# Pooled attention and a gated layer on one core: the first tile written in another order, value loads ahead of queries, the gate ahead of the second batch's value sums

## The chip, the cores and the metric

The kernel runs on one core of a Trainium2 chip. The metric is the device time of one execution in microseconds; lower is better. Three runs of the kernel before took 976.91 to 977.65, with a median of 977.51. The engines are TensorE (PE in the profile; its weight loads are PEld), VectorE (DVE), ScalarE (ACT), GpSimd (POOL) and SyncE (SP), which here issues all DMAs in the order of its list.

## What is computed

Eight batches of eight heads with 576 queries of 64 numbers. Keys and values are first averaged in groups of eight, to 72 each; the attention's output is the input x (4608 tokens of 512) of a gated layer with 1536 hidden columns.

```python
def _attn_ref(q, k, v):
    k_p = k.reshape(B, H, Sp, pool, D).mean(axis=3)
    v_p = v.reshape(B, H, Sp, pool, D).mean(axis=3)
    scores = scale * np.matmul(q, k_p.transpose(0, 1, 3, 2))
    scores = scores - np.max(scores, axis=-1, keepdims=True)
    attn = np.exp(scores)
    attn = attn / (np.sum(attn, axis=-1, keepdims=True) + 1e-09)
    return np.matmul(attn, v_p)

def _moe_ref(x, w_gate, w_val, w_out):
    g = x @ w_gate
    silu = g * (1.0 / (1.0 + np.exp(-g)))
    val = x @ w_val
    return silu * val @ w_out
```

## The kernel before

The tokens are worked through in nine tiles of 512. Tile 0 is batch 0's first 512 tokens; tile 1 is its last 64 and 448 of batch 1. A tile is made of pieces of at most 128 tokens of one batch: pieces 0 to 3 are tile 0, pieces 4 to 8 tile 1. The gated layer goes over the hidden columns in 12 chunks of 128. Products are taken in split precision: x and the gate and value weights each as a high and a low half-precision part, three products instead of one.

Tiles from 1 on are laid out by a planner (`hidden_tiles`), which puts attention work of later tiles between the matmuls of the present one. Tile 0 has no earlier work to hide behind, so its order, with that of all loads, weight preparation and attention of pieces 0 to 8, is written out by hand in `ORDER`: a list of job names with an index, recorded under a manual schedule, so that each engine gets its instructions in the order of the list, and waits for data by semaphores alone. One step (the last projection, O14) is issued behind it.

The jobs that this text names, with the engine that does them:

- Loads, on SP: `Lk`, `Lr` keys of batch 0 and 1 (halves, 576 KB), `Lv`, `Lu` values of batch 0 and 1 (parts 0 and 1 of the main rows, part 2 the rest, 512 KB), `Lq` queries of a piece (256 KB), `Lw` a weight chunk (1536 KB). `T` is a DMA transpose of a piece's softmax. `La` loads a part of batch 2.
- Attention of a piece: `S` scores (PE, L536), `M` subtract the row maximum (DVE, L552, L553), `E` exponential (ACT, L560), `Na` row sums (DVE), `N` normalise (POOL, L587), `H` and `P` high and low half (ACT, POOL), `T`, `Y` values (PE, L646 to L649), `X` and `Z` high and low half of x (ACT L669, DVE L673).
- Keys and values of a batch: `Kp`, `Kq`, `Kb` key sums (DVE, POOL L272 to L274); `Vp`, `Vq` value sums of batch 0 and 1 (PE, L381, into one PSUM bank); then `Vm` the largest (DVE), `Vo` its sum over rows (PE), `Vs` the scale, `R` ratios, `Vg`, `Vh` (DVE) and `Vx`, `Vf` (ACT) split them into halves.
- A weight chunk: `a` shift (DVE, L202), `b` sign (ACT, L212, or for three chunks DVE), `c` absolute value (ACT, L218), `d` join (DVE, L222), `e` sums (ACT, L233), `f` their total (PE, L181, L182), `g` scale (DVE), `h`, `j` high halves of gate and value weight (ACT, L248), `i`, `k` low halves (DVE, L253), `l`, `m` the output weight (ACT, POOL), `un` factors (POOL).
- The gated layer, step by step: `G` gate and `V` value side (PE, L797 to L799, 12 matmuls each), `t` tanh, `u` and `v` products, `w` cast, `y` low part, `O` projection (PE). Steps 0 to 2 are chunks 0 to 2 for the first 256 tokens, 3 to 5 the same chunks for the other 256, 6 to 14 chunks 3 to 11 for all 512. So steps 0 to 2 need x of pieces 0 and 1 alone.
- `ZERO` clears the four accumulators with zero matmuls (L937); `D` followed by a number is as many matmuls with zeros that change nothing (L941).

Small buffers turn: two for weight chunks as loaded (a third load waits until `d` of the first is done), two for queries, three for joined weights and batch parts, and two PSUM banks for everything of attention beside scores of pieces 0 to 3. Batch 1's value sums hold one of these two banks until they are split.

Of the kernel before, what the change touches and what calls it, by code (L numbers as in the profile page):

```python
# [34 lines left out]


ORDER = """
Lk0 Lq0 Lk1 Lv2 Lv1 Lv0 Lq1 Lw0 Kp0 Kb0 Kp1 CZ Lw1 Lr0 Lu0 S0 Vp0 M0 Lq2 Vp2 E0 Na0 S1
a0 N0 b0 Vp1 Lq3 M1 Vm0 a1 Vo0 E1 Vs0 Kq0 R0 Vx0 H0 Vh0 Vq0 b1 Vg0 S2 Lr1 Na1 Lu2 P0 S3
Lq4 Vf0 M2 N1 T0 Lq5 H1 Kq1 Vq2 E2 c0 Y0 Lu1 Na2 X0 d0 Z0 Lw2 P1 l0 Vq1 e0 M3 T1 m0 f0  # L40
c1 N2 g0 ZERO Vm1 h0 Vo1 E3 d1 H2 j0 Vs1 Lw3 P2 e1 R1 D10 Y1 Vg1 Vx1 T2 a2 X1 l1 Vh1 un0
b2 m1 Z1 D8 f1 g1 k0 S4 i0 a3 G0 h1 Lq6 j1 M4 un1 c2 V0 k1 t0 Y2 E4 d2 b3 Lw4 i1 Na3 u0
l2 N3 D8 G1 v0 X2 w0 c3 y0 m2 Z2 O0 t1 d3 H3 V1 e2 u1 Lw5 P3 v1 l3 f2 g2 e3 T3 a4 h2 f3
j2 g3 un2 i2 w1 j3 y1 h3 k2 D4 O1 b4 i3 G2 k3 a5 V2 b5 t2 Y3 c4 u2 m3 X3 v2 Vf1 Z3 d4 G3
w2 c5 y2 Lw6 un3 t3 O2 l4 d5 e4 V3 u3 Lw7 m4 l5 f4 G4 v3 g4 w3 m5 y3 j4 O3 e5 k4 V4 Na4
t4 c6 u4 N4 f5 G5 v4 g5 h4 w4 a6 S5 H4 y4 t5 un5 b6 i4 V5 Lq7 u5 P4 M5 O4 G6 v5 T4 un4
a7 w5 c7 y5 d6 E5 O5 t6 j5 u6 Lw8 S6 e6 k5 Na5 V6 h5 Lq8 M6 l6 N5 H5 i5 f6 G7 v6 E6 P5
g6 w6 h6 y6 j6 T5 a8 O6 t7 u7 un6 Na6 c8 S7 b8 b7 V7 M7 i6 G8 E7 v7 d7 w7 Y4 y7 Lw9 N6
e7 O7 t8 d8 H6 X4 u8 Lw10 m6 Y5 e8 Z4 V8 l8 k6 X5 m8 l7 Z5 c9 f7 f8 v8 m7 G9 g7 w8 g8 j7
un7 y8 j8 un8 a9 h7 V9 t9 Na7 b9 u9 N7 O8 v9 i7 k7 w9 H7 y9 G10 k8 c10 d9 h8 V10 t10  # L50
Lw11 i8 e9 u10 La0 a10 l9 f9 O9 v10 m9 g9 w10 h9 y10 j9 un9 O10 i9 b10 k9 La1 a11 G11
b11 d10 V11 t11 Pa0 l10 u11 e10 G12 v11 w11 y11 c11 m10 f10 O11 g10 t12 d11 h10 j10 u12
l11 un10 V12 k10 e11 i10 m11 La2 G13 v12 P6 w12 y12 f11 O12 t13 g11 P7 T6 u13 h11 j11 T7
k11 S8 Ln i11 un11 Pa2 V13 M8 La3 E8 G14 La4 Na8 v13 N8 w13 y13 Y6 Pa3 t14 u14 V14 X6
Pa4 H8 La5 P8 O13 v14 La6 w14 T8 y14 Z6 Pa5 Y7 Pa6 Y8 X7 Z7 X8 La7 Pa1 Z8 Pa7 A A
"""
# [1087 lines left out]
```

## Time and profile before

| | us |
|---|---|
| median of 3 runs | 977.51 |
| the profiled execution | 975.54 |
| its span, first to last instruction | 973.8 |
| PE busy in the span | 939.7 |
| DVE busy | 566.0 |
| ACT busy | 461.2 |
| POOL busy | 241.3 |

The profile is one execution. Its span is 1.74 us shorter than that execution's own time, and the execution is 1.97 us below the median of the runs. PE is busy 97% of the span; busy time alone does not say where the rest lies, so the rows below look at stretches.

### The profile page before, as it was taken

To read this page: it belongs to the slowest core of one execution; us is meant where nothing else is said; L and a number is where in the kernel's file an instruction comes from. 1 tells how busy PE (TensorE), PEld (TensorE's weight loads), DVE (VectorE), ACT (ScalarE), POOL (GpSimd) and SP (SyncE) were. 2 spreads that over 40 slices of the span, in tenths; PEclk is the share of its full clock that TensorE was granted. 3 is DMA by queue.
4 is the path that set the end of the run, shared out by engine and by line. 5 is a ranking of instruction groups with operands and counts; after the bars stand their busy time and mean duration, and the time that the engine had idled before them with its cause. 6 is when DMAs were issued, how large, how long until landed. Compare 5 with 4: busy or idle time off the path is not lost.

```text
span 973.8 us, 14306 instructions
## 1 busy us (share of the span) xinstructions
PE 939.7 (97%) x5486; PEld 498.4 (51%) x5486; DVE 566.0 (58%) x1005; ACT 461.2 (47%) x864; POOL 241.3 (25%) x327
## 2 busy tenths in 40 slices
PE   5779999799999999999999999999999999999998
PEld 4657545354555555554555555554545555444443
DVE  6788877667766675586446675674444454323222
ACT  3898883245554553544254544552454443222222
POOL 4533336035226230521025211620121201000000
PEclk9899999999999999999999999999999999999999
DMA  9855426246437342653047232840231222001001
GB/s 349 237 154 208 154 109 171 80 115 186 92 109 211 102 83 79 187 127 82 13 88 235 57 70 87 251 86 15 77 83 43 71 66 55 11 1 44 0 1 44
DMA packets 155524, 103.02 MB, mean 106 GB/s; under 512 B 113216, under 2 KB 141888, under 8 KB 153920
## 3 DMA queue, kind: packets, MB, share of 16 engines
q1 hardware_dynamic: 155456, 102.11, 37.3%
q8 instruction: 43, 0.70, 0.3%
q14 instruction: 25, 0.20, 0.1%
HBM read 67.63 MB, written 9.44 MB: 79 GB/s over the span
## 4 chain that ended last, share of the span: by engine, by line
PE 87%; DMA 6%; POOL 2%; ACT 2%; issue 1%; DVE 1%; SPq 0%; POOLq 0%; DVEq 0%; ACTq 0%
PE gv L797 18%; PE gv L798 18%; PE gv L799 18%; PE acc L824 10%; PE acc L830 9%; PE acc L831 9%; DMA pt<-half 2%; DMA kr<-k_rows 1%; DMA in<-v_rest 1%; DMA in<-k_rows 1%; PE ps L542 1%; PE ps L658 1%; PE ps L543 1%; PE ps L659 1%; DMA k<-k_rows 1%
## 5 line engine op out<-in xcount | busy, mean ns | idle before, releaser
L797 PE MATMUL gv<-x,wgv_h 128*128 128x512 f16 (+1 forms) x888 | 332.0, 374 | 3.8 <-ACT x L669 1.8
L798 PE MATMUL gv<-x,wgv_h 128*128 128x512 f16 (+1 forms) x888 | 331.8, 374 | 1.3 <-DVE x L673 1.3
L799 PE MATMUL gv<-x,wgv_l 128*128 128x512 f16 (+1 forms) x888 | 331.9, 374 | 0.5 <-DVE wgv_l L253 0.5
L810 DVE SCALAR_TENSOR_TENSOR hf<-hf,gv 128x512 f32<-128x512 f32 (+1 forms) x111 | 74.1, 668 | 171.6 <-ACT hf L807 171.3
L807 ACT ACTIVATE hf<-gv,un 128x512 f32<-128x512 f32 (+1 forms) x111 | 74.8, 674 | 193.9 <-PE gv L799 193.9
L1076 ACT CAST hh<-gv 128x512 fp32r<-128x512 f32 x96 | 56.3, 586 | 227.2 <-DVE gv L815 227.2
L831 PE MATMUL acc<-hb,wo_l 128*128 128x512 bf16 x384 | 145.5, 379 | 0.0
L824 PE MATMUL acc<-hh,wo_h 128*128 128x512 f32 (+1 forms) x444 | 139.5, 436 | 0.0
L799 PEld LDWEIGHTS <-wgv_l 128*128 128x128 f16 x888 | 87.0, 98 | 102.2 <-issue 1.7
L798 PEld LDWEIGHTS <-wgv_h 128*128 128x128 f16 x888 | 87.0, 98 | 98.1 <-issue 4.7
L797 PEld LDWEIGHTS <-wgv_h 128*128 128x128 f16 x888 | 87.4, 98 | 94.3
L1080 DVE TENSOR_TENSOR hl<-gv,hh 128x512 bf16<-128x512 f32 x96 | 66.3, 691 | 111.0 <-ACT hb L1077 111.0
L525 POOL TENSOR_TENSOR box<-qt,box 64x512 f16<-64x512 f32 (+1 forms) x60 | 64.0, 1067 | 227.8 <-issue 160.9
L815 DVE SCALAR_TENSOR_TENSOR gv<-gv,un,hf 128x512 f32<-128x512 f32 (+1 forms) x111 | 82.3, 741 | 63.0 <-PE gv L799 62.3
L830 PE MATMUL acc<-hl,wo_b 128*128 128x512 bf16 x288 | 109.8, 381 | 0.0
L824 PEld LDWEIGHTS acc<-hh,wo_h 128*128 128x128 f32 x444 | 83.2, 191 | 24.2 <-ACT hh L969 0.3
L630 POOL TENSOR_TENSOR half<-sc,half 128x512 f16<-128x512 f32 (+1 forms) x30 | 34.7, 1158 | 215.8 <-ACT half L620 193.6
L831 PEld LDWEIGHTS <-wo_l 128*128 128x128 bf16 x444 | 43.7, 98 | 37.9
L1077 ACT CAST hb<-gv 128x512 bf16<-128x512 f32 x96 | 56.8, 591 | 0.0
L830 PE MATMUL acc<-hl,wo_h 128*128 128x512 bf16 (+1 forms) x156 | 56.7, 368 | 0.0
L830 PEld LDWEIGHTS <-wo_b 128*128 128x128 bf16 x288 | 28.3, 98 | 42.2 <-issue 16.6
L523 ACT ACTIVATE qt<-qt,inv 128x512 f32<-128x512 f32 (+1 forms) x60 | 40.9, 682 | 0.0
(143 smaller groups left out, 1121.5 us busy)
## 6 DMA issues: line engine op xcount, KB each, us to landing
ws<-w_all SPq DMA_DIRECT2D x12, 1536.0 KB, 7.1
qt<-q_twice SPq DMA_DIRECT2D x48, 256.0 KB, 3.2
out_t<-ob SPq DMA_DIRECT2D x36, 256.0 KB, 2.3
in<-k_rows SPq DMA_DIRECT2D x12, 576.0 KB, 3.9
in<-q_rows SPq DMA_DIRECT2D x12, 576.0 KB, 5.2
in<-v_main SPq DMA_DIRECT2D x12, 512.0 KB, 4.3
in<-v_rest SPq DMA_DIRECT2D x12, 512.0 KB, 5.7
qt<-q_rows SPq DMA_DIRECT2D x8, 256.0 KB, 4.3
```

Of the source, the lines that this page charges most:

```text
L525: nc.gpsimd.tensor_sub(o[rows], qt[rows], o[rows])
L797: nc.tensor.matmul(o, wh, x["h"][:, j, a:e], start=(j == 0), stop=False)
L798: nc.tensor.matmul(o, wh, x["l"][:, j, a:e], start=False, stop=False)
L799: nc.tensor.matmul(o, wl, x["h"][:, j, a:e], start=False, stop=(j == NJ - 1))
L807: nc.scalar.activation(hf, gate, AF.Tanh, scale=un[:, c, 0:1])
L810: nc.vector.scalar_tensor_tensor(out=hf, in0=hf, scalar=1.0, in1=gate, op0=ALU.add, op1=ALU.mult)
L815: nc.vector.scalar_tensor_tensor(out=out, in0=val, scalar=un[:, c, 2:3], in1=hf, op0=ALU.mult, op1=ALU.mult)
L824: nc.tensor.matmul(o, wo_h[:, c, js], hh[:, :n], start=begin, stop=False)
L830: nc.tensor.matmul(o, wo[:, c, js], hl[:, :n], start=False, stop=False)
L831: nc.tensor.matmul(o, wo_l[:, c, js], hb[:, :n], start=False, stop=end)
L1077: nc.scalar.copy(hb[:, :n], val)
L1080: nc.vector.tensor_sub(hl[:, :n], val, hh[:, :n].bitcast(F32))
```

## The change

`ORDER` is written anew. It holds the same jobs, with one more (`Vc1`) and 24 idle matmuls instead of 30. The scores of piece 1 and batch 0's value loads come earlier, queries and one half of batch 1's keys (`Lr0`) later; pieces 0 and 1 are normalised and split before batch 1's key sums; the first gate (`G0`) stands ahead of the second batch's scale and split, and of the first score of piece 4. `Vc1` (`v_keep`) copies batch 1's value sums from PSUM to SBUF on ScalarE; what reads them afterwards reads the copy.

```diff
 ORDER = """
-Lk0 Lq0 Lk1 Lv2 Lv1 Lv0 Lq1 Lw0 Kp0 Kb0 Kp1 CZ Lw1 Lr0 Lu0 S0 Vp0 M0 Lq2 Vp2 E0 Na0 S1
-a0 N0 b0 Vp1 Lq3 M1 Vm0 a1 Vo0 E1 Vs0 Kq0 R0 Vx0 H0 Vh0 Vq0 b1 Vg0 S2 Lr1 Na1 Lu2 P0 S3
+Lk0 Lk1 Lv0 Lq0 Lq1 Lv2 Lw0 Lv1 Kp0 Kb0 Kp1 CZ Lw1 S0 Lu0 Lu1 S1 Lq2 M0 Vp0 Lq3 E0 Na0
+Vp2 N0 H0 M1 Vp1 a0 E1 Vm0 b0 Na1 Vo0 Vs0 N1 R0 Vq0 P0 Vg0 H1 Vf0 Vq1 Lr1 a1 T0 Vx0 P1
...
+    def v_keep(b):
+        kept = at.tile([P, NJ + 2, D], F32, name="vkept", bufs=1)
+        nc.scalar.copy(kept, state["vs", b])
+        state["vs", b] = kept
...
-            "Vm": v_largest, "Vo": v_total, ...
+            "Vc": v_keep, "Vm": v_largest, "Vo": v_total, ...
```

What this does to each engine is seen from the instructions in order. TensorE at its start, before (L381 are value sums, `v` batch 0's main part, `vr` any other part; L536 are scores, eight matmuls in 64 rows of keys each):

```order
L536 MATMUL ps<-ksum_122,qt 128x72 x8
L381 MATMUL ps<-v_145,unit 128x128 x8
L381 MATMUL ps<-vr,unit 128x128 x8
L536 MATMUL ps<-ksum_122,qt 128x72 x8
L381 MATMUL ps<-v_145,unit 128x128 x8
L181 MATMUL ps<-least,ones 128x1
L182 MATMUL ps<-mx_240,ones 128x1
```

and after:

```order
L541 MATMUL ps<-ksum_122,qt 128x72 x16
L381 MATMUL ps<-v_141,unit 128x128 x8
L381 MATMUL ps<-vr,unit 128x128 x8
L381 MATMUL ps<-v_141,unit 128x128 x8
L181 MATMUL ps<-least,ones 128x1
L182 MATMUL ps<-mx_243,ones 128x1
```

The scores of piece 1 (the second eight L536, now L541) moved ahead of all value sums.

SP from batch 1's second half of keys to the second load of the later chunks, before (`pt` is a transposed piece, `ws` a weight chunk, `vr` a value part, `kr` keys of batch 1):

```order
L286 DMA kr<-k_rows 128x1152
L372 DMA vr<-v_left 128x1024
L509 DMA qt<-q_rows 128x4x64
L637 DMA_TRANSPOSE pt<-half_132 128x10x128
L509 DMA qt<-q_rows 128x4x128
L372 DMA vr<-v_main 128x1024
L197 DMA ws<-w_all 128x3072
L637 DMA_TRANSPOSE pt<-half_133 128x10x128
L197 DMA ws<-w_all 128x3072
L637 DMA_TRANSPOSE pt<-half_132 128x10x128
L509 DMA qt<-q_rows 128x4x128
L197 DMA ws<-w_all 128x3072 x2
```

and after:

```order
L286 DMA kr<-k_rows 128x1152
L642 DMA_TRANSPOSE pt<-half_132 128x10x128
L372 DMA vr<-v_left 128x1024
L642 DMA_TRANSPOSE pt<-half_133 128x10x128
L514 DMA qt<-q_rows 128x4x64
L514 DMA qt<-q_rows 128x4x128
L197 DMA ws<-w_all 128x3072 x2
L642 DMA_TRANSPOSE pt<-half_132 128x10x128
L514 DMA qt<-q_rows 128x4x128
L286 DMA kr<-k_rows 128x1152
L642 DMA_TRANSPOSE pt<-half_133 128x10x128
L197 DMA ws<-w_all 128x3072
```

The transposes of pieces 0 and 1 moved ahead of chunk 2 (the first `ws` here) and of queries; piece 3's transpose (the second `half_133`) moved ahead of chunk 4, and the first half of batch 1's keys behind piece 2's.

ScalarE from the second sign pass (L212) to the high halves of chunk 0 (L248), before (`half_133` is piece 1's softmax, `wf` joined weights, `sc` a score tile):

```order
L212 ACTIVATE ws<-ws 128x1536
L432 ACTIVATE vst_f_130<-fh,mask 128x2x64 x4
L600 CAST half_133<-sc 128x512
L602 CAST half_133<-sc 128x2x32 x2
L560 ACTIVATE sc<-sc 128x576
L218 ACTIVATE wf<-ws 128x1536
L669 ACTIVATE x<-ps,r 128x4x128
L259 CAST wo_h<-wf 128x512
L233 ACTIVATE wgv_h,wm<-wf 128x512 x2
L218 ACTIVATE wf<-ws 128x1536
L248 ACTIVATE wgv_h<-wf,sw 128x512
```

and after:

```order
L212 ACTIVATE ws<-ws 128x1536
L565 ACTIVATE sc<-sc 128x576
L674 ACTIVATE x<-ps,r 128x4x128
L218 ACTIVATE wf<-ws 128x1536 x2
L388 COPY vkept<-ps 128x384
L233 ACTIVATE wgv_h,wm<-wf 128x512 x2
L259 CAST wo_h<-wf 128x512
L674 ACTIVATE x<-ps,r 128x4x128
L565 ACTIVATE sc<-sc 128x576
L248 ACTIVATE wgv_h<-wf,sw 128x512 x2
```

Piece 1's casts moved ahead of the sign pass, the absolute value of chunk 1 (the second L218) and the new copy ahead of chunk 0's sums (L233), and x of piece 1 (the second L674) ahead of its high halves.

## Rows read from the trace of the kernel before

**Rows 1.** Windows: us; busy us of PE, PEld, DVE, ACT, POOL (instructions); clock; DMA.

```profile
0.00:25.00 25.00, 13.38 (x100) 12.41 (x100) 15.22 (x40) 8.57 (x10) 10.88 (x25) 1.00 0.93 346
25.00:50.00 25.00, 19.26 (x156) 14.89 (x156) 18.73 (x41) 21.03 (x34) 12.54 (x17) 0.86 0.84 225
50.00:77.00 27.00, 21.38 (x162) 16.63 (x160) 22.87 (x36) 26.24 (x40) 7.87 (x10) 0.87 0.57 150
77.00:171.00 94.00, 93.44 (x586) 53.86 (x584) 75.10 (x121) 68.32 (x112) 42.12 (x53) 1.00 0.51 165
```

**Rows 2.** Timeline of PE: start us, us, operation, [idle before it <- releaser].

```profile
17.54 1.11 PE L536 MATMUL ps<-ksum,qt 64*128 64x72 f32 x16
...
42.73 0.23 PE L646 MATMUL ps<-pt,vst_h 128*128 128x128 f16 x1 [2.71 <-DMA pt<-half]
...
49.28 0.28 PE L799 MATMUL gv<-x,wgv_l 128*128 128x256 f16 x1 [0.48 <-DVE wgv_l L253]
...
70.67 0.22 PE L646 MATMUL ps<-pt,vst_h 128*128 128x128 f16 x1 [0.55 <-DMA pt<-half]
...
72.51 0.27 PE L797 MATMUL gv<-x,wgv_h 128*128 128x256 f16 x1 [0.78 <-ACT x L669]
73.30 0.27 PE L798 MATMUL gv<-x,wgv_h 128*128 128x256 f16 x1 [0.52 <-DVE x L673]
```

**Rows 3.** Timeline of SP, the queue that issues the DMAs.

```profile
33.63 0.33 SPq L197 DMA_DIRECT2D ws<-w_all  x1
34.02 3.30 SPq L637 DMA_TRANSPOSE pt<-half  x1
...
54.22 6.96 SPq L197 DMA_DIRECT2D ws<-w_all  x2
62.13 2.84 SPq L637 DMA_TRANSPOSE pt<-half  x1
```

**Rows 4.** Timeline of POOL.

```profile
26.63 1.15 POOL L587 TENSOR_TENSOR sc<-sc,ri 128x576 f32<-128x576 f32 x1 [0.45 <-DVE ri L583]
27.74 1.40 POOL L272 TENSOR_TENSOR kr<-kr 128x576 f32<-128x576 f32 x1
```

**Rows 5.** DMA issues by line: count, KB each, median us from issue to landing.

```profile
ws<-w_all SPq DMA_DIRECT2D x12, 1536.0 KB, 7.1
```

**Rows 6.** Timeline of DVE.

```profile
16.65 0.96 DVE L202 TENSOR_SCALAR ws<-ws 128x1536 uint32<-128x1536 uint32 x1 [1.91 <-DMA ws<-w_all]
...
20.67 0.56 DVE L328 TENSOR_REDUCE mx<-ps 128x1 f32<-128x384 f32 x1 [0.18 <-PE ps L381]
...
54.11 0.74 DVE L253 SCALAR_TENSOR_TENSOR wgv_l<-wf,sw,wgv_h 128x512 f16<-128x512 f32 x1
...
87.09 0.45 DVE L552 TENSOR_REDUCE mx<-ps 128x4 f32<-128x288 f32 x1
```

**Rows 7.** Timeline of ACT.

```profile
17.65 3.64 ACT L212 ACTIVATE ws<-ws 128x1536 f16<-128x1536 f32 x1 [4.14 <-DVE ws L202]
...
35.31 0.19 ACT L233 ACTIVATION_READ_ACCUMULATOR wgv_h<-wf 128x1 f32 x1
...
50.22 1.59 ACT L218 ACTIVATE wf<-ws 128x1536 f32<-128x1536 f32 x1
```

**Rows 8.** Groups by line and form to 185 us: count | busy us, mean ns | idle before.

```profile
L838 ACT COPY ob<-acc 128x512 f32<-128x512 f32 x2 | 1.2, 587 | 3.0 <-DVE box L267 1.6 <-PE ps L649 1.4
L669 ACT ACTIVATE x<-ps,r 128x256 f16<-128x256 f32 x2 | 0.9, 474 | 0.0
```

**Rows 9.** Timeline of PE, from tile 0 to tile 1.

```profile
171.44 0.19 PE L646 MATMUL ps<-pt,vst_h 128*128 128x64 f16 x1 [0.85 <-DMA pt<-half]
173.14 0.38 PE L797 MATMUL gv<-x,wgv_h 128*128 128x512 f16 x1 [1.06 <-ACT x L669]
174.26 0.38 PE L798 MATMUL gv<-x,wgv_h 128*128 128x512 f16 x1 [0.75 <-DVE x L673]
...
184.22 0.35 PE L181 MATMUL ps<-least,ones 128*128 128x3 f32 x2 [2.39 <-DVE sc L553]
```

More of the change, by code (lines that the diff above doesn't have):

```diff
@@ L37 @@
 ORDER = """
-Lk0 Lq0 Lk1 Lv2 Lv1 Lv0 Lq1 Lw0 Kp0 Kb0 Kp1 CZ Lw1 Lr0 Lu0 S0 Vp0 M0 Lq2 Vp2 E0 Na0 S1
-a0 N0 b0 Vp1 Lq3 M1 Vm0 a1 Vo0 E1 Vs0 Kq0 R0 Vx0 H0 Vh0 Vq0 b1 Vg0 S2 Lr1 Na1 Lu2 P0 S3
[L40 to L55, printed above, removed]
+Lk0 Lk1 Lv0 Lq0 Lq1 Lv2 Lw0 Lv1 Kp0 Kb0 Kp1 CZ Lw1 S0 Lu0 Lu1 S1 Lq2 M0 Vp0 Lq3 E0 Na0
@@ new lines @@
+Vp2 N0 H0 M1 Vp1 a0 E1 Vm0 b0 Na1 Vo0 Vs0 N1 R0 Vq0 P0 Vg0 H1 Vf0 Vq1 Lr1 a1 T0 Vx0 P1
+b1 S2 Vh0 Lu2 S3 T1 M2 Kq1 Lq4 Lq5 M3 E2 Y0 X0 Vq2 Z0 c0 Na2 ZERO d0 c1 Y1 Vc1 Lw2 d1 e0
+l0 f0 Vm1 Lw3 N2 X1 g0 E3 Z1 Vo1 h0 un0 Na3 j0 e1 i0 D4 G0 k0 a2 l1 D8 f1 V0 t0 g1 H2 u0
+un1 j1 v0 P2 h1 Vs1 w0 R1 S4 Vx1 y0 T2 m0 Vg1 b2 Vh1 Lq6 O0 m1 M4 N3 c2 Y2 i1 H3 k1 D6
+G1 X2 a3 E4 V1 Lr0 t1 Z2 P3 b3 u1 v1 T3 d2 w1 Kq0 Lw4 e2 y1 D6 O1 l2 f2 Vf1 g2 Y3 Na4 j2
+X3 k2 h2 Z3 N4 c3 S5 a4 H4 Lq7 M5 P4 b4 S6 T4 i2 d3 G2 E5 M6 V2 Lw5 l3 un2 m2 Lq8 t2 e3
@@ new lines @@
+u2 Y4 Na5 c4 f3 G3 v2 N5 g3 w2 j3 y2 d4 t3 O2 h3 X4 V3 E6 u3 Lw6 m3 Z4 e4 G4 v3 k3 w3 l4
+f4 y3 t4 i3 V4 c5 u4 m4 g4 G5 h4 v4 a5 w4 j4 O3 t5 y4 un4 u5 c6 un3 O4 a6 V5 b5 b6 G6 v5
+d5 w5 H5 y5 Lw7 k4 l5 O5 e5 i4 V6 d6 t6 u6 Lw8 P5 l6 e6 f5 G7 v6 g5 w6 T5 m6 h5 y6 c7 O6
+i5 a7 t7 j5 u7 un5 b7 k5 V7 a8 b8 Y5 f6 G8 X5 v7 m5 Z5 w7 g6 c8 y7 un6 d7 O7 t8 h6 u8
+Lw9 l7 d8 e7 S7 j6 Lw10 i6 V8 e8 M7 m7 l8 k6 E7 f7 f8 G9 v8 Na7 w8 c9 y8 N7 g7 V9 t9 g8
+un7 j7 u9 un8 h8 a9 h7 O8 j8 v9 m8 w9 y9 b9 i7 O9 a10 i8 k8 G10 b10 k7 Na6 V10 d9 t10
@@ L56 @@
+c10 u10 Lw11 N6 La0 S8 Ln v10 l9 d10 w10 G11 H6 y10 P6 l10 e10 V11 t11 M8 T6 m10 e9 m9
+u11 E8 O10 v11 H7 a11 w11 y11 P7 f9 f10 O11 g9 g10 h9 T7 un9 j10 i9 h10 j9 k10 Y6 i10
+G12 X6 k9 c11 b11 La1 V12 t12 d11 u12 Y7 l11 un10 Pa1 Z6 e11 G13 v12 w12 X7 y12 La2 m11
+f11 Z7 O12 t13 g11 u13 h11 un11 j11 i11 V13 k11 Na8 La3 N8 G14 v13 w13 Pa2 H8 y13 V14
+t14 La4 P8 u14 O13 v14 Pa3 T8 w14 y14 Pa4 La5 Pa0 La6 Y8 La7 X8 Z8 Pa5 Pa6 Pa7 A A
 """
@@ L996, in first_tile @@
             "Vp": lambda g: v_sum(0, g), "Vq": lambda g: v_sum(1, g),
-            "Vm": v_largest, "Vo": v_total, "Vs": v_scale, "Vx": v_high, "Vh": v_low, "Vg": v_left, "Vf": v_spread,
+            "Vc": v_keep, "Vm": v_largest, "Vo": v_total, "Vs": v_scale, "Vx": v_high, "Vh": v_low, "Vg": v_left, "Vf": v_spread,
             "R": ratio, "ZERO": lambda _: zero(), "D": idle, "CZ": lambda _: fields(), "Kb": lambda _: k_last(),
```

## The prediction

> **What bounds the kernel now.** I first cut the run into stages by the view of windows, which gives each engine's busy time in a stretch [rows 1]. TensorE is busy 13.38 of the first 25 us, 19.26 of the next 25 and 21.38 of the 27 up to 77 us; from 77 to 171 us it is busy 93.44 of 94. So 11.62 + 5.74 + 5.62 = 22.98 us of idle TensorE lie ahead of 77 us, and after that it is the bound. In the two stretches between 25 and 77 us its granted clock is 0.86 and 0.87, so some of its work there ran at the lower level. The instructions behind the first tile stand in the same order in both kernels, so the change can win or lose only in those first 77 us and where the first tile hands over to the second.
>
> Then I read TensorE's timeline there, for what ended each wait [rows 2]. The scores of piece 1 (S1) start at 17.54, behind two value sums. The values of piece 1 (Y1) wait 2.71 us for a transpose, until 42.73. The first gate (G0) waits for VectorE's low weight until 49.28. Y3 and G3 then wait 0.55, 0.78 and 0.52 us. Last I looked at who was late for Y1. On SP, piece 1's transpose (T1) is issued only at 34.02, behind a weight chunk (Lw2, 33.63) [rows 3], and its source is late because GpSimd puts a sum of the second batch's keys (27.74) between normalising piece 1 (26.63) and its low part [rows 4].
>
> **The change part by part.** I number the time by the trace of before, and keep every duration from it.
>
> *Front of the tile.* S1 now stands directly behind S0, which needs the same keys as before. Queries come later in the load order, values earlier, so S0 stays near 9.5 to 10.7 us and S1 ends near 12. Piece 1's exponential can then go near 16.5. Its sum on VectorE stands behind the largest value of batch 0 (Vm0), which needs the value part Lv1, now behind Lw0: 2 x 576 + 3 x 512 + 2 x 256 + 1536 = 4736 KB are loaded up to its end, as many as up to Lw0's end before, which VectorE first touched at 16.65 [rows 6]. From S1's end (18.65) to Vm0's start (20.67) one part's value sums took 2.0, and Vm0 0.56 [rows 2, 6]: 19.3. With piece 1's row sums behind it, N1 runs near 20.5 instead of 26.63 [rows 4]. GpSimd then does P0 and P1 at once, the key sums later, and SP can issue T1 near 25 instead of 34.02. T1 took 8.71 us to Y1 behind Lw2 [rows 2, 3]; now Lu2 alone is ahead of it, and Lw2 is behind. I take 5 to 6: pt lands near 31, and Y1 follows Vq2 and the four zeroing matmuls near 33. That is 10 us sooner.
>
> *The gate.* G0 needs more than x: chunk 0's weight must be scaled. Its sums on ScalarE end at 35.50 [rows 7]. In the new order ScalarE does both sign passes (3.64 us each) [rows 7], c0, c1 and the new copy ahead of those sums. Counting along its list from piece 0's exponential on, I come to 35 for the sums, 37.5 for the high half and 38.6 for the low. So G0 moves from 49.28 to about 38.6, and its value side ends near 43.3 instead of 51.7 (49.28 and 22 matmuls 0.11 apart). From here the weights are late, no longer x.
>
> *The copy (Vc1).* The trace has no ScalarE copy of 128x384 from PSUM. A 128x256 took 474 ns and a 128x512 587 [rows 8]; I take 0.53 us, and both ends change nothing. It stands on ScalarE while that engine sets the end, so it counts in full; it frees a PSUM bank for f0 near 34, instead of after the second batch's split.
>
> *What remains of the lead.* ScalarE is busy 26.24 of the 27 us from 50 to 77 [rows 1], so it cannot give back 10 us. Up to c2 its list before ended at 50.22 + 1.59 = 51.8 [rows 7]. The new list holds the same work and a tanh, a cast and the copy beside, and ends near 50. That is a lead of 2 us and those three, some 3 us of work. Next comes a chain through the loads: chunk 2's join (d2) ends near 56, which frees the buffer for Lw4; a chunk takes 7.1 us to land [rows 5]; then, in VectorE's order, a4 (0.96), piece 5's maxima (four instructions of 0.45) and chunk 2's low gate weight (0.74) [rows 6] give 66.6, and with the hops 66.8 for G2. Before, G2, V2 and a gap of 0.55 ended at 70.67, where Y3 starts [rows 2]; the two sides take 24 x 0.107 = 2.6 (256 columns at 2.4 GHz) and the drain 0.2, so G2 started near 67.3. The head start of ten has shrunk to 0.5. But by then TensorE has also done Y3 (some 1.0), S5 and S6 (1.11 each, as S1), which stood behind G2 [rows 2], and not yet f3 (small sums, some 0.3). First term: 0.5 + 3.2 - 0.3 = 3.4 us. Its bounds: 0, if the chain is 3.4 us longer; 8.4, the lead of V0, if nothing holds it.
>
> *Behind G2.* The waits of 0.55 + 0.78 + 0.52 = 1.85 us at Y3 and G3 go [rows 2], since x of the second half is ready. Late next is ScalarE's cast for O2, near 72 against G3's end near 72, so I expect a new wait of about 1.3. Second term: 0.5, between -1.3 and 1.85.
>
> *Fillers.* Idle matmuls (D) fall from 30 to 24, 0.21 us each (512 columns at 2.4 GHz): 1.3 us at most, counted as 0, since all lie in front of something late. Here a note speaks against the change. In the rows the clock is below 1 in just the two stretches in which TensorE waits among its matmuls [rows 1]. The Trainium skill ("TensorE: Matmul & The Clock Gate", section "Why this matters for your kernels") says that gaps between bursts of matmuls bring the clock back to half. By that rule fewer fillers would leave G2 to V3 at the lower level, and the sum would come out some 4 us smaller; by the rows, which show such spells before as well, it stays. The rule's case is a rival below.
>
> *The handover.* Y8 now stands ahead of the last projection (O14), not behind it. Before, Y8 waited 0.85 us for its transpose and tile 1's first gate 1.06 and 0.75 more for x [rows 9]: 2.66 us. O14's 3 us now cover that. But the loads and sums of batch 2's queries then come just before tile 1's first gated product on VectorE, and the wait of 2.39 us at 184.22, for a PSUM bank that VectorE frees, stays as it is [rows 9]. Third term: 1.5, between 0 and 2.66.
>
> The sum is 3.4 + 0.5 + 1.5 = 5.4 us. The profiled execution took 975.54 us (span 973.8 and 1.74 around it), 1.97 below the median of the three, 977.51. So I expect 970.1 for a run like it, and 972.1 for the median.
>
> **The rivals.** *The whole lead is kept:* ScalarE's order may carry more than I think, as from 77 to 171 us it is busy 68.32 of 94 [rows 1]. Against it: the chain through Lw4. Price: 8.4 + 2.66 - 1.0 for new waits, 10 us, 967.5. Chance 0.13.
>
> *The clock eats it:* TensorE waits several times between G0 and G2 (for two PSUM banks at S4 and S5, for w0 and w1), and then runs G2, V2 and G3 at the lower level. A side of 12 such matmuls takes 1.3 us at 2.4 GHz, and as long again at half. Three sides and a projection cost 4 to 5 us, which leaves 0.5 to 1.5: 976.5. For it: clocks of 0.86 and 0.87 [rows 1]. Against it: before pays this as well. Chance 0.13.
>
> *Slower, by SP's queue:* Lw4 stood ahead of T3 (54.22 against 62.13) [rows 3] and now stands behind it, and Lw5 behind T4. SP takes its list in order, so a late T3, which waits for two GpSimd passes behind the cast of its softmax (H3), holds the fourth chunk, and through a4 and the maxima also G2. I put T3 near 52, 4 us ahead of d2, so it costs nothing; from 56 on each us costs one. At T3 = 64, two us behind where it stands today, Lw4 lands near 72 and G2 starts near 75: 8 us lost, 2.6 after the sum, 980. Chance 0.1.
>
> *The gate isn't early at all:* if Lu2 or the copy is late, f0 has no bank, and G0 comes near 47, which leaves the handover and 1 us: 975. By my count the bank is free some 1.5 us before f0. Chance 0.06.
>
> **How the numbers follow.** My forecast, a gain of 3 to 7.5 us (970 to 974.5), has the remaining 0.58. This kernel's runs tell some 0.2% (2 us) from no change. Faster by more: 0.58 + 0.13 + 0.06 and a little of the clock case, 0.80. Within: most of the clock case, 0.11. Slower: 0.09. The range runs from the kept lead to the clock case, 967 to 977.5, and leaves out the slower one.
>
> **What would show it.** G0 near 38 to 40 and V0's end near 43; Y1 near 33; T1 issued near 25; G2 between 64 and 69 with S5, S6 and Y3 ahead of it; a clock below 1 only before about 72; no wait at Y8, and tile 1's first gate near 168 to 169 instead of 173.14; the wait of 2.4 us for the sums still there. I am wrong if T3 is issued behind 56, if G2 starts behind 71, or if TensorE shows idle stretches between 77 and 165.

## The result and the profile after

The changed kernel takes 982.21 us (median of 12 runs, 978.44 to 984.18), the kernel before 976.53 in the same comparison (12 runs, 974.51 to 979.72). The ratio is 1.005, with an interval of 1.0035 to 1.0065: slower by some 5 us, where 972.1 was forecast. The profiled execution of after took 983.38 us, its span is 981.6; that is 7.84 above the profiled execution of before, of which 2 to 3 are the spread of single executions.

Windows of after, in the columns of [rows 1], with two more stretches at the end:

```profile
0.00:25.00 25.00, 14.77 (x109) 14.50 (x110) 15.05 (x41) 8.49 (x12) 10.45 (x24) 1.00 0.91 344
25.00:50.00 25.00, 19.03 (x162) 14.90 (x161) 19.32 (x39) 21.14 (x35) 11.89 (x16) 0.86 0.69 203
50.00:77.00 27.00, 18.32 (x128) 13.77 (x128) 18.61 (x34) 21.27 (x29) 12.59 (x12) 0.72 0.36 119
77.00:171.00 94.00, 92.03 (x573) 54.11 (x572) 76.09 (x119) 73.34 (x119) 36.48 (x47) 0.99 0.55 163
171.00:185.00 14.00, 13.53 (x87) 7.02 (x85) 11.76 (x13) 2.82 (x5) 4.13 (x6) 1.00 0.82 229
185.00:200.00 15.00, 11.98 (x45) 5.47 (x43) 6.69 (x17) 3.40 (x6) 0.00 (x0) 0.77 0.04 13
```

The last two stretches of before, not shown so far:

```profile
171.00:185.00 14.00, 9.36 (x68) 4.96 (x69) 9.36 (x16) 2.72 (x5) 0.00 (x0) 1.00 0.35 123
185.00:200.00 15.00, 15.00 (x71) 7.30 (x69) 9.81 (x20) 4.69 (x10) 1.49 (x2) 1.00 0.14 30
```

From such rows a ledger can be made. TensorE's lost time in a stretch is its idle time (the width less the busy time), and the time lost to the lower clock, which is the busy time multiplied by one less the granted clock (in tile 1 the gate's 512-column matmuls of after start 0.43 us apart behind 190.79, and 0.22 apart behind 195.13):

| us | idle before | idle after | clock loss before | clock loss after |
|---|---|---|---|---|
| 0 to 25 | 11.62 | 10.23 | 0 | 0 |
| 25 to 50 | 5.74 | 5.97 | 2.70 | 2.66 |
| 50 to 77 | 5.62 | 8.68 | 2.78 | 5.13 |
| 77 to 171 | 0.56 | 1.97 | 0 | 0.92 |
| 171 to 185 | 4.64 | 0.47 | 0 | 0 |
| 185 to 200 | 0 | 3.02 | 0 | 2.76 |
| sum | 28.18 | 30.34 | 5.48 | 11.47 |

The difference is 2.16 of idle time and 5.99 of clock, 8.15 together, against 7.84 measured. (The stretches 171 to 200 must be read together, because after stands 4 to 5 us behind there.) In this pair of profiles most of the loss is TensorE running at the lower of its levels, 1.2 GHz instead of 2.4, in the stretch from 50 to 77 us and behind one wait in tile 1.

That division is coarse, and it is of one pair. With windows of half a microsecond in place of the six stretches, the clock loss is 6.8 and 12.0, a difference of 5.2. And profiles of runs described below, which have the same list up to `G9`, divide it otherwise. Up to 77 us:

| profile | list up to `G9` | idle | clock loss | sum | G2 starts |
|---|---|---|---|---|---|
| before | before | 22.98 | 5.48 | 28.46 | 67.33 |
| `e3` | before | 23.20 | 4.52 | 27.72 | 67.64 |
| `e8` | before | 23.00 | 5.71 | 28.71 | 68.92 |
| after | after | 24.88 | 7.79 | 32.67 | 76.25 |
| `e4` | after | 24.24 | 7.51 | 31.75 | 73.51 |
| `e7` | after | 26.45 | 5.60 | 32.05 | 75.67 |

So a loss of 3 to 5 us up to 77 us stands clear of the spread, but its division does not: in `e7` the clock takes no more than in before, and all of the loss there is idle time. The 2.76 us in tile 1 are a high value too; seven other profiles, with waits of 2.87 to 3.07 us at the same place, lose 1.3 to 1.7 there. And the start of one instruction is known from one profile only to some 3 us.

TensorE's timeline of after, with what answers to [rows 2] first and to [rows 9] in the last four lines:

```profile
32.05 3.78 PE L381 MATMUL ps<-vr,unit 128*128 128x128 f32 x16 [2.19 <-DMA vr<-v_left]
...
37.33 0.31 PE L651 MATMUL ps<-pt,vst_h 128*128 128x128 f16 x1
...
40.58 0.27 PE L802 MATMUL gv<-x,wgv_h 128*128 128x256 f16 x1
...
41.89 0.28 PE L804 MATMUL gv<-x,wgv_l 128*128 128x256 f16 x1 [0.92 <-DVE wgv_l L253]
...
42.99 1.89 PE L946 MATMUL acc<-zeros 128*128 128x512 f16 x8
...
45.08 0.27 PE L802 MATMUL gv<-x,wgv_h 128*128 128x256 f16 x1
...
53.49 0.29 PE L651 MATMUL ps<-pt,vst_h 128*128 128x128 f16 x1 [1.65 <-DVE sc L558]
...
55.18 2.77 PE L946 MATMUL acc<-zeros 128*128 128x512 f16 x6
57.74 0.42 PE L802 MATMUL gv<-x,wgv_h 128*128 128x256 f16 x1
...
63.76 0.74 PE L829 MATMUL acc<-hh,wo_h 128*128 128x256 f32 x4 [1.70 <-ACT hh L974]
...
68.73 1.98 PE L541 MATMUL ps<-ksum,qt 64*128 64x72 f32 x14 [1.69 <-DVE x L678]
73.47 0.67 PE L541 MATMUL ps<-ksum,qt 64*128 64x72 f32 x2 [2.76 <-issue]
...
76.25 0.40 PE L802 MATMUL gv<-x,wgv_h 128*128 128x256 f16 x1
...
174.62 0.20 PE L651 MATMUL ps<-pt,vst_h 128*128 128x64 f16 x1 [0.47 <-DMA pt<-half]
...
177.91 0.38 PE L802 MATMUL gv<-x,wgv_h 128*128 128x512 f16 x1
...
188.71 0.56 PE L181 MATMUL ps<-least,ones 128*128 128x3 f32 x2 [3.02 <-DVE sc L558]
...
190.79 0.63 PE L802 MATMUL gv<-x,wgv_h 128*128 128x512 f16 x1
```

The same gate starts of before (G0, G1 and G2):

```profile
48.42 0.28 PE L797 MATMUL gv<-x,wgv_h 128*128 128x256 f16 x1
...
56.30 0.27 PE L797 MATMUL gv<-x,wgv_h 128*128 128x256 f16 x1 [1.80 <-ACT ws L212]
...
67.33 0.27 PE L797 MATMUL gv<-x,wgv_h 128*128 128x256 f16 x1
```

Y1 is at 37.33 (before 42.73). G0 starts at 40.58 and gets its first low weight at 41.89, where before had 48.42 and 49.28: the gate is 7 to 8 us early. V0 starts at 45.08, behind eight idle matmuls and f1, and ends near 46.4. Then comes Y2's wait (53.49) with six idle matmuls behind it, and G1 starts at 57.74, where before had 56.30: the lead is gone. With waits at O1 (63.76), S5 (68.73) and S6 (73.47), G2 starts at 76.25, 9 us later than in before. Tile 1's first gate no longer waits, but the sums of batch 2 do, for 3.02 us, and the gate matmuls behind them take 0.63 us instead of 0.38.

VectorE of after (u1, d2, a4 and i2), the engine of [rows 6]:

```profile
60.00 0.42 DVE L815 SCALAR_TENSOR_TENSOR hf<-hf,gv 128x256 f32<-128x256 f32 x1 [2.86 <-ACT hf L812]
...
61.21 1.75 DVE L222 SCALAR_TENSOR_TENSOR wf<-wf,ws 128x1536 uint32<-128x1536 uint32 x1
...
70.78 1.66 DVE L202 TENSOR_SCALAR ws<-ws 128x1536 uint32<-128x1536 uint32 x1 [2.10 <-DMA ws<-w_all]
...
74.14 0.74 DVE L253 SCALAR_TENSOR_TENSOR wgv_l<-wf,sw,wgv_h 128x512 f16<-128x512 f32 x1
```

ScalarE of after (the copy, the high halves of chunk 1, c2, t1 and b4), the engine of [rows 7]:

```profile
35.86 0.48 ACT L388 COPY vkept<-ps 128x384 f32<-128x384 f32 x1 [1.46 <-PE ps L381]
...
45.71 1.33 ACT L248 ACTIVATE wgv_h<-wf,sw 128x512 f16<-128x512 f32 x2 [1.19 <-DVE sw L190]
...
51.89 1.61 ACT L218 ACTIVATE wf<-ws 128x1536 f32<-128x1536 f32 x1
...
59.50 0.47 ACT L812 ACTIVATE hf<-gv,un 128x256 f32<-128x256 f32 x1 [2.82 <-PE gv L804]
...
72.48 3.63 ACT L212 ACTIVATE ws<-ws 128x1536 f16<-128x1536 f32 x1 [1.78 <-DVE ws L202]
```

SP of after (T1, T3 and the load Lw4), the queue of [rows 3]:

```profile
27.74 1.35 SPq L642 DMA_TRANSPOSE pt<-half  x1
...
57.78 1.35 SPq L642 DMA_TRANSPOSE pt<-half  x1
62.98 0.33 SPq L197 DMA_DIRECT2D ws<-w_all  x1
```

c2 ends at 53.5, not near 50; d2 starts at 61.21, behind u1, which waits 2.86 us for the tanh of G1; the load of chunk 4 goes out at 62.98, and a4 waits for it until 70.78.

### The profile page after: what moved, and what is told of

Same layout as the page of the kernel before. It is cut to its first block, busy times and chain, and to the rows that moved or that the text cites. A ratio compares the mean times of both kernels' runs of the same rounds, so it can differ in the third digit from the quotient of the medians.

```text
span 981.6 us, 14291 instructions
## 1 busy us (share of the span) xinstructions
PE 945.0 (96%) x5480; PEld 501.7 (51%) x5480; DVE 569.0 (58%) x1005; ACT 462.3 (47%) x865; POOL 243.1 (25%) x327
## 4 chain that ended last, share of the span: by engine, by line
PE 86%; DMA 5%; DVE 5%; ACT 1%; issue 1%; POOL 1%; SPq 0%; DVEq 0%; POOLq 0%; ACTq 0%
PE gv L802 17%; PE gv L804 17%; PE gv L803 17%; PE acc L829 9%; PE acc L835 9%; PE acc L836 9%; DMA ws<-w_all 2%; PE ps L381 2%; DMA in<-k_rows 1%; DVE wf L222 1%; PE ps L547 1%; PE ps L663 1%; PE ps L548 1%; PE ps L541 1%; PE ps L664 1%
```

## The experiments

Three theories. **A:** TensorE waits because chunk 2's weight is late, through the order of the lists on ScalarE, VectorE and SP. **B:** another order only shifts the waits. **C:** the lower clock behind the waits costs the time. All ratios are to the kernel before, run on the same chip.

**The two ends of the list.** `e3` takes the list of before up to G9 and that of after behind it, without the copy; `e4` the other way round.

```diff
-(all of before's ORDER)
+(before's ORDER up to G9) (after's ORDER behind G9)
```

> The order of before up to G9, and from there the changed order for what is left of tile 0, without the copy. If the handover is better in the changed order (Y8 ahead of the last projection, third term of the prediction), the waits of 0.85, 1.06 and 0.75 us at the start of tile 1 go and the time falls by 1.5 to 2.7 us below before, to about 974.5. If the tail gains nothing (the wait for the sums of batch 2 grows as much, 3.0 us instead of 2.4 in the changed kernel, and the clock falls behind it), the time is that of before, 976.5, or up to 2 us above.

Measured: 975.62 (971.78 to 977.68, one run of 1589 us aside), ratio 0.9982 (0.9967 to 0.9996).

```profile
169.21 0.20 PE L651 MATMUL ps<-pt,vst_h 128*128 128x64 f16 x1 [0.49 <-DMA pt<-half]
172.49 0.38 PE L802 MATMUL gv<-x,wgv_h 128*128 128x512 f16 x1
183.15 0.35 PE L181 MATMUL ps<-least,ones 128*128 128x3 f32 x2 [2.87 <-DVE sc L558]
```

> The changed order up to G9, then the order of before for the rest of tile 0. If the loss lies in the front (theories A, B and C), this has all of it and lacks the better handover: 1.5 to 2.7 us above the changed kernel, about 984. If the loss lay in the tail (wait for batch 2's sums and the lower clock behind it), it comes out 2 us or more below the changed kernel, near 979 or less.

Measured: 988.92, ratio 1.0134 (1.0113 to 1.0154). Six jobs of before's front had to be put in at the seam, and a wait of 3.33 us there is the seam's own. `e3` says that the new tail gains some 1.7 us by itself (0.4 to 3.2 by the interval). So the loss of the changed kernel lies in the front, or in what the front does to the tail; `e4`, with the seam in it, agrees but adds little.

**One late step at a time.** `e1` moves chunk 2's join ahead of u1:

```diff
-... b3 u1 v1 T3 d2 w1 ...
+... b3 d2 u1 v1 T3 w1 ...
```

> One job moved in the changed order: chunk 2's join (d2) stands ahead of the first product of step 1 (u1) instead of behind its second (v1), so that the buffer for weight chunk 4 comes free earlier. Theory A (the late fourth chunk holds G2: its load is issued at 62.98 behind d2, and VectorE's a4, piece 5's maxima and i2 follow it): the load goes near 59, a4 no longer waits, G2 starts near 73.5 instead of 76.25, and the time falls by 2 to 3 us, to about 979.5. Theory B (the block of VectorE work of batch 1 ahead of piece 4's maxima is what costs, the chunk is hidden behind it): G2 stays within 1 us of 76, and the time within 1 us of 982. Theory C (TensorE at the lower clock is the cost): no change either.

Measured: 982.39, ratio 1.0052 (1.0032 to 1.0072). d2 starts at 57.70 and ends 3.2 us sooner, Lw4 goes out only 1.6 us sooner, at 61.37, behind T3 (59.94), which stands ahead of it on SP; G2 starts at 74.94, and nothing is gained. `e2` moves the second batch's split (R1, Vx1, Vg1, Vh1) behind Z2 or E4, so that O0 and Y2 come sooner:

```diff
-... Vs1 w0 R1 S4 Vx1 y0 T2 m0 Vg1 b2 Vh1 Lq6 O0 ... E4 V1 Lr0 t1 Z2 P3 ...
+... Vs1 w0 S4 y0 T2 m0 b2 Lq6 O0 ... E4 Vx1 V1 Lr0 t1 Z2 R1 Vg1 Vh1 P3 ...
```

> In the changed order batch 1's ratios and split (R1, Vg1, Vh1 on VectorE, Vx1 on ScalarE) stand behind Z2 instead of ahead of y0 and piece 4's maxima; the scale Vs1 stays where it is. Theory B (this block of some 6 us on VectorE holds O0 by 2.0 us and, through the PSUM bank, Y2 by 1.65): both waits go, Y2 starts near 51 instead of 53.5 and G1 near 53 to 54 instead of 57.7, and all behind it comes 3 to 4 us earlier: about 978.5. Theory A alone: d2, and with it chunk 4, moves with G1, so the gain is the same 3 us; if the block is only moved and VectorE is short of time later, G2 stays near 76 and the time at 982. Theory C (the clock): Y2 and the idle matmuls behind it, which ran at the lower level, keep it, and less than 1 us is gained.

Measured: 981.54, ratio 1.0044 (1.0019 to 1.0068). The wait of 2.01 us inside O0 is gone, Y2 starts at 51.35, and the time comes back in one piece at O1:

```profile
61.21 0.73 PE L829 MATMUL acc<-hh,wo_h 128*128 128x256 f32 x4 [3.58 <-ACT hh L974]
```

`e9` does chunk 3's sign pass on VectorE, to clear ScalarE ahead of w1 and e2:

```diff
-SIGN_AS_INT = (5, 8, 11)
+SIGN_AS_INT = (3, 5, 8, 11)
```

> The changed kernel with chunk 3's sign pass (b3, 3.63 us on ScalarE) done on VectorE (about 1.9 us), in the same place of the order; VectorE idles 2.86 us there. Theory A (ScalarE's list, in which w1 and chunk 2's sums e2 stand behind b3 and b3 behind the second gate's tanh, sets O1 and G2): O1 loses its wait of 1.70, e2 ends about 3 us sooner, G2 starts near 73 instead of 76.25, and the time falls by 2 to 4 us, to 978 to 980. Theory B (VectorE, the loads and the PSUM banks of S5 and S6 hold G2 by themselves): O1 comes sooner, but S6 waits as much longer, G2 stays within 1 us of 76, and the time within 1.5 us of 982.

Measured: 982.54, ratio 1.0065 (1.0047 to 1.0083). O1's wait falls to 0.92, S5's grows from 1.69 to 2.72, and G2 starts at 76.00. Theory B's numbers.

**G2 where the forecast had it.** `e5` puts all of chunk 2's preparation ahead of chunk 3's and of the scores S5 and S6:

```diff
-t1 Z2 P3 b3 u1 v1 T3 d2 w1 Kq0 Lw4 e2 y1 D6 O1 l2 f2 Vf1 g2 ... h2 Z3 N4 c3 S5 a4 ... i2 d3 G2
+t1 Z2 d2 P3 Lw4 e2 u1 v1 T3 w1 Kq0 l2 y1 f2 D6 g2 O1 h2 j2 Vf1 ... i2 Z3 N4 D4 G2 b3 S5 V2 ...
```

> The changed kernel with another list from the second gate step on: chunk 2's join, sums, scale and halves (d2, e2, f2, g2, h2, i2) stand ahead of chunk 3's sign pass (b3), of the low part of chunk 4 (a4) and of the scores of pieces 5 and 6 (S5, S6, M5, M6), which move behind G2; b4, f3 and chunk 3's halves move behind G3 with them. Theory A (what was late is chunk 2's weight, because its preparation stands in ScalarE's and VectorE's lists behind work that waits for the early gate or is not needed yet): G2 starts near 65 instead of 76.25, TensorE's idle time from 50 to 80 us falls by at least 3 us, and the time falls by 5 to 8 us, to 974 to 977. Theory B (the first tile's loads and ScalarE are so full that another order only shifts the wait): G2 comes sooner, but G6 or a step behind it waits for chunk 3 or 4 as long, and the time stays within 2 us of 982. Theory C (TensorE's clock after waits is the main loss): the time falls only as far as the stretch at the lower level gets shorter, 2 to 3 us.

Measured: 992.36, ratio 1.015 (1.0123 to 1.0176). G2 starts at 72.01, but Y3 waits 4.66 us for the transpose that now stands behind Lw4, and the sums of chunk 3 come late:

```profile
94.36 0.59 PE L182 MATMUL ps<-wm,ones 128*128 128x2 f32 x2 [5.55 <-ACT wgv_h L233]
```

`e13` leaves chunk 3 in its place, and puts G2 and V2 ahead of S5 and S6, and i2 ahead of a4:

```diff
-h2 Z3 N4 c3 S5 a4 H4 Lq7 M5 P4 b4 S6 T4 i2 d3 G2 E5 M6 V2 ... t2 e3 u2 Y4 Na5 c4 f3 G3
+h2 i2 Z3 N4 G2 c3 V2 H4 un2 t2 S5 a4 Lq7 u2 M5 P4 b4 v2 d3 G3 S6 T4 ... O2 f3
```

> The changed kernel with the third gate step (G2, V2) ahead of the scores of pieces 5 and 6 (S5, S6), and chunk 2's low gate weight (i2) ahead of the shift of chunk 4 (a4), so that G2 waits neither for the load of chunk 4, nor for the PSUM banks of piece 5's and 6's scores; t2, u2, G3 follow in the same spirit, ahead of b4, f3 and Y4. Chunk 3 stays where it is. Theory A (what made G2 late is the chain d2, load of chunk 4, a4, maxima of piece 5, and the scores that stand ahead of it): G2 starts near 69 instead of 76.25, the waits of 1.69 and 2.76 us at S5 and S6 are gone or filled with G2, V2 and G3, and the time falls by 3 to 6 us, to 976 to 979. Theory B (chunks 3 and 4 set the pace, so the waits come back at G4 to G7): G2 at 69, but a wait or a later V9, and the time within 1.5 us of 982.

Measured: 984.51, ratio 1.0071 (1.0045 to 1.0097). G2 on TensorE's timeline:

```profile
67.05 0.31 PE L802 MATMUL gv<-x,wgv_h 128*128 128x256 f16 x1 [1.80 <-ACT wgv_h L248]
```

and its windows:

```profile
50.00:77.00 27.00, 20.56 (x158) 14.94 (x157) 17.46 (x31) 20.19 (x31) 12.06 (x11) 0.81 0.33 107
77.00:171.00 94.00, 90.02 (x538) 52.22 (x543) 76.39 (x119) 73.46 (x118) 40.46 (x51) 0.98 0.55 166
```

This is the run that decides on the forecast's first term. G2 starts at 67.05, where 66.8 was forecast, though without S5 and S6 done ahead of it. By 77 us the ledger stands 3.8 us better than after's (23.64 idle and 5.20 of clock, against 24.88 and 7.79). But from 77 to 171 us, 3.98 idle and 1.80 of clock stand against 1.97 and 0.92, and the time is no shorter. (Up to 200 us the ledger is still 2.5 better, and the two profiled executions took the same time; it closes only to some 2 us.) One of the new waits is for the sums of chunk 3, at 84.51:

```profile
84.51 0.38 PE L182 MATMUL ps<-wm,ones 128*128 128x2 f32 x2 [0.93 <-ACT wgv_h L233]
```

**The early gate undone.** `e11` keeps the loads, the copy and the new order, and moves G0 to O0 back behind the second batch's split:

```diff
-D4 G0 k0 a2 l1 D8 f1 V0 t0 g1 H2 u0 ... Vh1 Lq6 O0 m1 M4 N3 c2 Y2
+D4 k0 a2 l1 D8 f1 g1 H2 ... Vh1 G0 Lq6 m1 M4 N3 c2 V0 t0 Y2 i1 H3 k1 u0 D6 G1 v0 ... O0 V1
```

> The changed kernel with the early gate undone: the front, the loads and the copy stay, but G0 moves from behind the first chunk's low weight to behind the second batch's split (Vh1), V0 behind chunk 2's absolute value (c2), and tanh, products, casts and O0 as far behind, so that O0 stands behind Z2 and V1 follows it. If the early gate is what cost the time (its tanh, casts and products stand in ScalarE's and VectorE's lists ahead of the weight work of chunks 2 to 4, and these wait for TensorE): V9 ends 3 us or more sooner than the 128.05 of the changed kernel, and the time falls to 977 to 979. If the rest of the new order is (loads, piece 4 and the bank that its maxima hold, the scores ahead of G2): within 1.5 us of 982 or above.

Measured: 980.03, ratio 1.0038 (1.0021 to 1.0054). V9 ends at 127.72 against 128.05, and the interval overlaps the changed kernel's (1.0035 to 1.0065): at most a part of the loss is the early gate's. The waits at Y2 (3.71), S5 (2.72) and S6 (2.97) stand without it.

**The clock by itself.** `e6` puts 36 more idle matmuls into waits of the first tile, `e7` 12 ahead of batch 2's sums in tile 1; in both nothing else moves.

```diff
-... c2 Y2 ... D6 O1 ... S5 ... S6
+... c2 D8 Y2 ... D14 O1 ... D8 S5 ... D12 S6
```

> The changed kernel with 36 more idle matmuls in TensorE's waits of the first tile: 8 ahead of Y2, 8 more ahead of O1, 8 ahead of S5, 12 ahead of S6 (0.21 us each at the higher clock, so 1.7 to 2.5 us in waits of 1.65, 1.70, 1.69 and 2.76 us). Nothing else moves. Theory C (the lower clock behind these waits costs the time): the granted clock from 68 to 80 us rises from 0.5 to near 1, G2 and V2 take 2.8 us instead of 4.0, and the time falls by 2.5 to 4 us, to 978 to 980. Theory A (only the waits for chunk 2's weight count): G2 starts at 76 as before, and the time falls by no more than 1.2 us, or rises where the idle matmuls themselves are late.

Measured: 978.94, ratio 1.0014 (1.0000 to 1.0028). Its window answers to the third line of after's:

```profile
50.00:77.00 27.00, 25.73 (x202) 16.73 (x201) 20.74 (x39) 22.95 (x35) 12.32 (x12) 0.94 0.43 130
```

The clock is 0.94 instead of 0.72. G2 starts at 72.67 instead of 76.25 and a4 at 68.67 instead of 70.78, but this can't be put down to the idle matmuls: `e4`, which has the changed list there without them, has a4 at 68.74 and G2 at 73.51.

```profile
73.51 0.40 PE L802 MATMUL gv<-x,wgv_h 128*128 128x256 f16 x1
```

The profiled execution of `e6` is the slowest of its twelve (982.46), so what the runs gained is not to be read from it; the gain is shown by the ratio, whose interval lies clear of the changed kernel's.

```diff
+        if b == SPLIT:
+            spare = now["acc"]()[0]
+            for _ in range(12):
+                nc.tensor.matmul(spare, zeros[:, :P], zeros, start=True, stop=True)
         sums = over_rows(mx[:, :3])
...
+            now["acc"] = acc
```

> The changed kernel with 12 idle matmuls (512 columns) just ahead of batch 2's sums in tile 1, where TensorE waited 3.02 us for a PSUM bank and then ran 18 matmuls of 512 columns in 6.6 us instead of 3.9. Nothing in the first tile moves. Theory C: the wait of 3.02 is filled, the 18 matmuls behind it run at the higher level, and the time falls by 2.2 to 3 us, to near 979.5. Rival (that stretch was slow for another reason, or is hidden): no change.

Measured: 980.21, ratio 1.0023 (1.0006 to 1.004), whose interval just overlaps the changed kernel's. TensorE's timeline there:

```profile
184.34 2.75 PE L493 MATMUL acc<-zeros 128*128 128x512 f16 x12
187.45 0.36 PE L181 MATMUL ps<-least,ones 128*128 128x3 f32 x2 [0.36 <-DVE sc L562]
...
188.54 0.38 PE L806 MATMUL gv<-x,wgv_h 128*128 128x512 f16 x1
```

The sums wait for the same bank as before, with idle matmuls in the wait, and the gate behind them takes 0.38 us a matmul instead of 0.63.

**Both, and a better version.** `e10` joins d2 early, the sign pass on VectorE, 30 idle matmuls in the first tile and the 12 in tile 1.

```diff
-... c2 Y2 ... u1 v1 T3 d2 ... D6 O1 ... S5 ... S6
+... c2 D8 Y2 ... d2 u1 v1 T3 ... D10 O1 ... D8 S5 ... D10 S6
```

> The changed kernel with four edits at once: chunk 3's sign pass on VectorE, chunk 2's join (d2) ahead of u1, idle matmuls in the first tile (8 ahead of Y2, 10 instead of 6 ahead of O1, 8 ahead of S5, 10 ahead of S6), and 12 ahead of batch 2's sums in tile 1. The idle matmuls of the first tile alone took 978.94 and those of tile 1 alone 980.21, from 982.21. Theory C (what the change lost is the clock, in these two places): their gains add up, 3.3 and 2.0 us, to near 977, level with the kernel before; with theory A as well, 2 us more, 975. If neither, 979 or more.

Measured: 975.30, ratio 0.9989 (0.9974 to 1.0004), by the ratios 6 us below the changed kernel. The two small edits had brought nothing when made alone (`e1`, `e9`), and the gains of `e6` and `e7` add up to as much (3.5 and 2.6 us by their ratios). `e14` adds to `e13` the early d2 and 18 idle matmuls in the first tile, with the 12 of tile 1:

```diff
-... c2 Y2 ... D6 O1 ... i2 Z3 N4 G2
+... c2 D8 Y2 ... D10 O1 ... i2 Z3 N4 D6 G2
```

> The same, and with it d2 ahead of u1, idle matmuls 8 ahead of Y2, 10 instead of 6 ahead of O1 and 6 ahead of G2, and 12 ahead of batch 2's sums in tile 1. If theory A and theory C (clock) both hold, their gains add up: 3 to 6 us from the order and some 4 from the idle matmuls, 972 to 975, below the 975.30 of the run with the join ahead and idle matmuls. If only C holds, 976 to 978.

Measured: 979.14, ratio 1.0021 (1.0003 to 1.004): no better than `e10`, which has 12 idle matmuls more and chunk 3's sign pass on VectorE, so no gain of the early G2 shows on top of the clock either. Its window from 77 to 171 us, in the slowest of its twelve executions (983.42):

```profile
77.00:171.00 94.00, 88.20 (x531) 51.17 (x535) 76.26 (x119) 72.90 (x117) 38.02 (x47) 0.98 0.53 161
```

It has 5.8 us of idle time, where after has 1.97, and 1.62 of it is again a wait for chunk 3's sums. `e8` and `e12` are before's front with after's tail and the 12 idle matmuls, `e12` with 20 more in the front:

```diff
-... V0 ... Y3 ... G3
+... D8 V0 ... D6 Y3 ... D6 G3
```

> The list of the kernel before up to G9, the changed kernel's list behind it (as in the run with front before and tail after), and the 12 idle matmuls ahead of batch 2's sums. That run without them took 975.93, with a wait of 2.87 at the sums and a clock loss of 1.7 us behind it. Theory C: 1.2 to 1.8 us less, near 974.4, and a ratio to the kernel before near 0.9965. Rival: 976, no change from that run.

Measured: 975.25, ratio 0.9978 (0.9963 to 0.9993).

> The list of the kernel before up to G9 and the changed kernel's behind it, with 12 idle matmuls ahead of batch 2's sums (975.25 in that form), and 20 more in the first tile's waits: 8 ahead of V0 (2.17 us), 6 ahead of Y3 (1.38) and 6 ahead of G3 (0.78 and 0.51). Theory C: the front's clock loss of some 7 us there shrinks by 1.5 to 3, the time falls to 972.5 to 974. Rival: what is filled was hidden, the idle matmuls themselves are late, and the time is 975 to 976.5.

Measured: 974.57, ratio 0.9976 (0.9961 to 0.9992). Both beat the two kernels, and neither can be told from `e3` (0.9982), so the gain there is the tail's. The idle matmuls gained nothing measurable on the old front; `e12`'s clock from 50 to 77 us is 0.94, but `e8` without the 20 had 0.92 there already (before 0.87). The forecast of 972.5 to 974 was a miss.

What the copy brings was not tried apart: without it f1 would wait for a bank whose release stands behind it in the list. Nor was a run made without the idle matmuls ahead of f1 and G1.

## Why the prediction was wrong

**The step that failed is the first term, "What remains of the lead"** (3.4 us, read at G2's start).

- Its chain was built as it is, but mis-timed. c2 was put near 50, and ends at 53.5 (51.9 to 53.5 in after, `e4` and `e7`; 51.8 to 54.3 in before, `e3` and `e8`): ScalarE has no lead left. From 31.31 to c2 it stands idle for 3.61 us in after: 1.46 ahead of the copy, which waits for the last value sums, 0.96 for other work of TensorE, and 1.19 for the scale of chunk 1, whose sums (f1) stand behind eight idle matmuls (42.99). The term has none of these waits. Behind c2, ScalarE is busy 21.27 of the 27 us from 50 to 77, against 26.24 [rows 1]. d2 was put to end near 56 and ends near 63, because u1 stands ahead of it and waits for the tanh of G1. Then S5 and S6, which the term counted as work already done, waited in front of G2. S6 waited 2.76 us, and went on 0.1 us after the first half of piece 5's maxima ended (73.37); the profile names no releaser there. The lower bound of 0 left out that the chain could come out 9 us later, as it did.
- And its conversion into time was wrong. `e13` started G2 at 67.05 and gained nothing; `e5` started it at 72.01 and lost 10 us more. From there to V9, other chunks, casts and transposes are late in G2's stead. So G2's start does not measure what the front is worth. That the rate of weight preparation is what lies behind it is borne out by the three runs that moved G2 ahead, in which TensorE then waits for chunk 3's sums (5.55 us in `e5`, 0.93 in `e13`, 1.62 in `e14`; no such wait in after), but not shown for every run.

**The rival "the clock eats it" is the other half of what happened, with a price too small.** I let it eat the gain (976.5), and held against it that before pays this as well. The ledger of one pair has the changed kernel paying 5.99 us more than before; by the other profiles it is some 1.5 in tile 1 and 0 to 3 up to 77 us, with longer waits for the rest. That the clock behind the waits costs time is shown by the runs: idle matmuls in waits, with nothing else changed, took the ratio from 1.005 to 1.0014 in the first tile and to 1.0023 in tile 1, and both together, with two edits that gain nothing alone, to 0.9989. On before's front they gained nothing measurable. The "Fillers" were counted at 0, because they stand in front of something late. Their worth lay behind them; and two groups do not stand in front of something late in after: V0 and G1 start straight behind f1 and the six idle matmuls (45.08, 57.74), with their weights ready at 42.5 and 55.6. The rule of the Trainium skill that was weighed there ("TensorE: Matmul & The Clock Gate", section "Why this matters for your kernels"), that gaps between bursts of matmuls bring the clock back to half, agrees with these traces at the longer waits: 0.63 us a matmul behind the wait of 3.02, 0.38 in `e7`; behind before's wait of 2.39 it stayed at 0.38. The rival deserved more than 0.13.

**The second term's waits went as forecast.** Y3 and G3 no longer wait, and the new wait at O2 did not come either; but S5 and S6 wait in front of G2 instead.

**The third term came out in size, but its neighbour did not stay as it was.** `e3` gives some 1.7 us where 1.5 was forecast; Y8's wait is 0.47, and the gate's 1.06 and 0.75 are gone. But the wait for the sums, said to stay as it is at 2.39, became 3.02 (2.87 in `e3`), since VectorE does a part of batch 2's keys and queries later, and the matmuls behind it fell to the lower level: 2.76 us of clock loss in 185 to 200.

**What came as forecast, or nearly.** The gate is early. (The 49.28 that the prediction moves is G0's third matmul, the first with a low weight; it came at 41.89 where 38.6 was forecast, and V0's end at 46.4 instead of 43.3.) The copy took 0.48 us (0.53; the 474 ns taken for it in [rows 8] is an activation, not a copy). T1 went out at 27.74 (near 25). T3 went out at 57.78 (near 52), yet the rival of SP's queue did not decide: Lw4 waited for d2; only in `e1` and `e14`, with d2 sooner, did it wait for T3. Y1 came at 37.33 instead of 33, behind the last value sums, which waited 2.19 us for their load.

All three signs of being wrong that the prediction names are in the trace: T3 behind 56, G2 behind 71, and idle TensorE between 77 and 165 us, 1.8 us in waits of 0.28 to 0.62, where before has 0.15.

**Open.** The first 77 us have 1.0 to 3.5 us more idle time than before's, and the stretch up to 171 some 1.4 more; `e11` gives back only a part, with intervals that overlap. Which of the moved loads, splits or scores makes the rest was not found. How much of the loss is idle time and how much the clock differs from profile to profile of the same list.

## What to carry to other kernels

Where every engine takes its list in order, a step that is written earlier makes its readers wait earlier, and the work behind them with it; ask what the stage as a whole lacks before counting a lead at one instruction. Make the ledger of idle time and clock loss by stretch before and after, from more than one profile of each list: a wait costs itself and the slow matmuls behind it, and here the loss of clock was mended by idle matmuls without touching the order. A gain at one point counts only if the next stretch does not give it back.
